# Operand sums, PSUM squares and weight portions in a kernel of attention and two feed-forward layers

## The chip, the cores and the metric

The kernel runs on one core of a Trainium2 chip. The metric is the device time of one execution in microseconds (us). TensorE (PE) multiplies matrices into eight PSUM banks, VectorE (DVE), ScalarE (ACT) and GpSimd (POOL) work element by element on SBUF and, the first two, on PSUM; SyncE (SP) issues DMAs.

## The reference

```python
def phi(x):                      # per batch and head, 128 random features
    proj = np.einsum('bhsd,md->bhsm', x, omega)
    h = proj - np.sum(x * x, axis=-1, keepdims=True) / 2.0
    h = h - np.max(h, axis=-1, keepdims=True)
    return np.exp(h) / np.sqrt(m)
kv = einsum(phi(k), v);  z = sum(phi(k))
attn = (phi(q) @ kv) / (phi(q) @ z + 1e-06)        # 4 x 8 heads, 576 x 64
x = attn as (2304, 512)
h = x @ moe_w_in;   r = maximum(h, 0); x = (r * r) @ moe_w_out      # 512 x 2048, 2048 x 512
h = x @ moe2_w_in;  g = where(h > 0, h, exp(minimum(h, 0)) - 1);  out = g @ moe2_w_out
```

All in float32.

## The kernel before

Each float32 operand is kept as two limbs of a shorter format, high and low, and each product is three matmuls (high x high, high x low, low x high). A low limb is made by VectorE as full minus high (`minus`, L76; names gl, wl, t1l and so on), the high one by a cast on ACT.

The 2304 tokens stand in five blocks: 0 to 3 of 512 columns and B = 4 of 256. The 2048 hidden columns of each layer stand in four groups of four (GF = 4). Group 0 of the first layer is computed plainly and partly beside the attention stages, in steps of one hidden part: blocks 0 to 2 in halves of 256 columns, then block 3, then block 4. Step s runs `gemm1` (12 matmuls into ph; ACT makes r = relu(ph), L516, and gh = r², L517; VectorE gf = r*r, L520, and gl = gf - gh) and then `gemm2` of step s - 2 (12 matmuls from gh and gl into py, L540). After the fourth part the sum py is copied to a page ya in SBUF by VectorE (L551, L557). Weight work is put between: `make(n, c)` carries weight part n through five phases: cm on ACT (L132), which reads a loaded page st; L139 and L140 on VectorE into cv; L149 on VectorE and, for pairs of parts, four sums cs and cd on GpSimd (L166 to L169); the cast wh on ACT (L195, L179); wl on VectorE.

All other groups are "tours" over one block each, with seven products in the manner of Strassen. A tour runs `product` (L662) into the PSUM pages pa, pw and pb; ACT copies pb, vs and us (L827, L828, L833) and VectorE adds c22 = pb + vs and c21 = pw + us (L839, L842); the squares follow (L676 to L678), then `chunk` (py, L721) and the sum into ya (L737). The products need sums of the input blocks: GpSimd joins the two limbs of x to xf (L620) and forms t1 to t4, and d for block B (L591 to L597); ACT and VectorE split each into limbs, SP stores these to DRAM (L571), and `load_x` brings them back. The tasks stand in a list `later`, of which `prepare(n)` takes n at fixed places of the program. The engines run their instructions in the program's order; the order is written out by hand.

Of the kernel before, what the change touches and what calls it, by code (L numbers as in the profile page):

```python
# [8 lines left out]
F32 = mybir.dt.float32  # L9
# [8 lines left out]
def linear_attention_two_ffn_kernel(  # L18
# [47 lines left out]
    def page(shape, name, dt=F32):  # L66
        return pages.tile([P] + list(shape), dt, tag="page", name=name)
# [4 lines left out]
    def flat(t):  # L72
        return t.rearrange("p a b -> p (a b)")
# [421 lines left out]
    def gemm1(o, j, ahead):  # L495
        i, n0, n1 = o
        n = n1 - n0
        nm = f"0_0_{i}_{n0}_{j}"
        ih, il = need((0, j, 0))
        lower()  # L500
        cast()
        ph = psum(f"ph{nm}")
        m = 0
        for c in range(KD):
            cs = slice(c * P, (c + 1) * P)
            for wt, xt in ((ih, xh), (ih, xl), (il, xh)):
                nc.tensor.matmul(ph[:, :n], wt[:, cs], x_part(xt, i, c)[:, n0:n1], start=(m == 0), stop=(m == 3 * KD - 1))  # L507
                m += 1
        if o == order(0, 0)[-1]:
            n_dead[0] += 1  # L510
        gf = page([n], f"gf{nm}")
        gh = page([n], f"gh{nm}", F32R)
        gl = page([n], f"gl{nm}", F32R)
        r = page([n], f"r{nm}")

        nc.scalar.activation(out=r, in_=ph[:, :n], func=AF.Relu)  # L516
        nc.scalar.activation(out=gh, in_=r, func=AF.Square)  # L517
        make(ahead, 1)
        make(ahead, 2)
        nc.vector.tensor_tensor(out=gf, in0=r, in1=r, op=ALU.mult)  # L520
        minus(nc.vector, gl, gf, gh)
        for c in (3, 0, 4):
            make(ahead, c)
        g_t[o, j] = gh, gl
        prepare(1)

    def gemm2(o, j):
        i, n0, n1 = o
        n = n1 - n0
        oh, ol = need((0, j, 1))  # L530
# [13 lines left out]
        if o == order(0, 0)[-1]:  # L544
            n_dead[0] += 1
        if j < GF - 1:
            return
        if per == 2:
            for t in range(KD // per):
                ya = ya_t[i, n0 // HN, t] = page([W], f"ya0_{i}_{n0}_{t}")  # L550
                nc.vector.tensor_copy(out=ya, in_=y_t[t])  # L551
            return
        for t in range(KD):
            for l in range(2):
                if t % 2 == 0:
# [46 lines left out]
    def operands1(i):  # L602
# [3 lines left out]
        made = [(name, b[l, k]) for name, l, k in PARTS[i == B]] + found  # L606
        later.extend(lambda name=name, t=t: split(1, i, name, t) for name, t in made)

    def operands0(i):

        def piece(d, l, k):
            return [x_part(d, i, 2 * k + e)[:, l * HN:(l + 1) * HN] for e in range(2)]

        def joined():
            b = {}
            for l in range(1 if i == B else 2):
                for k in range(2):
                    b[l, k] = page([W], f"xf{i}_{l}_{k}")
                    for e, (h, o) in enumerate(zip(piece(xh, l, k), piece(xl, l, k))):
                        nc.gpsimd.tensor_tensor(  # L620
                            out=b[l, k][:, e * HN:(e + 1) * HN], in0=h.bitcast(F32), in1=o.bitcast(F32), op=ALU.add
                        )
            found_t[i] = terms(0, i, b)

        for name, l, k in PARTS[i == B]:
            keep(0, i, name, (piece(xh, l, k), piece(xl, l, k)))
        joined()

    found_t = {}

    def operands0_limbs(i, n):
        name, t = found_t[i][n]
        split(0, i, name, t)

    def idle():
        pass

    def load_x(tour, name):
        moe, g, k, i = tour
# [110 lines left out]
        if moe == 0 and g == NG - 1 and l == (i < B):  # L750
            operands1(i)

    AHEAD = (0, 1, 3, 5, 8)

    def weights(tour):

        moe, g, k, i = tour
        prepare(2)
        lim = min(len(parts), 2 * NF * moe + 2 * GF * (g + 1) + AHEAD[k])
        due = n_made[2] - n_made[3]  # L760
        n_cast = len(casts)
        for _ in range(due):
            make(lim, 3)
        for _ in range(n_cast):
            cast()
        while n_made[1] < lim:
            make(lim, 0)
            make(lim, 0)
            make(lim, 1)
        for _ in range(due):  # L770
            make(lim, 4)
        for _ in range(n_cast):
            lower()
        while n_made[2] < lim:
            make(lim, 2)

    def toured(before):

# [5 lines left out]
        for n, tour in enumerate(tours):  # L784
# [6 lines left out]
            if i == B:  # L791
                bank_e, bank_o = psum(f"pe{nm}"), psum(f"po{nm}")
                times(tour, bank_e, "a", 0, "u", True, False, True)
                times(tour, bank_e, "a", 1, "v", False, True, False)
                run(carried)
                weights(tour)
                earlier(0)
                act_a(tour, "11", bank_e)
                times(tour, bank_o, "b", 0, "u", True, False, True)
                times(tour, bank_o, "b", 1, "d", False, True, False)  # L800
                earlier(1)
                act_a(tour, "21", bank_o)
# [4 lines left out]
                prepare(2)  # L807
# [22 lines left out]
            weights(tour)  # L830
# [5 lines left out]
            prepare(2)  # L836
# [8 lines left out]
            prepare(2)  # L845
# [120 lines left out]
```

## Time and profile before

| | |
|---|---|
| Median of three runs | 950.0 us (948.54 to 952.68) |
| Profiled execution | 950.98 us |
| Its span; granted clock of TensorE, mean | 949.1 us; 0.992 |
| PE busy | 917.3 us (97%) |
| DVE busy | 703.4 us (74%) |
| ACT busy | 528.9 us (56%) |
| POOL busy | 261.9 us (28%) |

Busy times are sums over a whole execution and hide in which stretch an engine is late; the waits and the stretches in the section of rows below do not. A matmul counts as busy until its modelled end, so that the number of matmuls in a stretch says more than its busy time. Durations are those of one profiled execution.

### The profile page before, as it was taken

The page shows a single profiled execution, that of the slowest core. Times are in us where ns is not written, and L with a number is a line of the kernel's source. Part 1 is how long each engine was busy: PE and PEld are TensorE (multiplying, and loading weights), DVE is VectorE, ACT ScalarE, POOL GpSimd, SP SyncE. Part 2 cuts the span into 40 slices and gives each one's busy share as a digit, 9 for nine tenths or more (in the row PEclk, how much of TensorE's full clock was granted, in tenths as well). Part 3 has the DMA queues.
Part 4 walks back from the last instruction along what each step waited for, and adds up shares of the span by engine and source line. Part 5 has one row for each costly group of instructions (what it writes and reads, how often), then busy time and mean ns, then how long its engine had stood idle before and what let it go on. Part 6 is the DMA issues. An engine that isn't in the chain of part 4 may idle for free.

```text
span 949.1 us, 20503 instructions
## 1 busy us (share of the span) xinstructions
PE 917.3 (97%) x7731; PEld 856.1 (90%) x7731; DVE 703.4 (74%) x1170; ACT 528.9 (56%) x1126; POOL 261.9 (28%) x370
## 2 busy tenths in 40 slices
PE   8998999969989999999999999999999999999997
PEld 7887889958889999999999998998899889989896
DVE  5889886899775775477549899897678767976553
ACT  5988966424343444254335565766476637665551
POOL 7666643589201100110025323220022002100000
PEclk9999999999999999999999999999999999999999
DMA  9464430345899685467439655376466746654632
GB/s 249 140 171 117 134 112 2 92 153 201 277 365 347 209 290 188 159 229 266 179 94 372 234 199 190 129 237 233 156 222 197 291 155 213 207 192 137 207 122 78
DMA packets 122882, 183.86 MB, mean 194 GB/s; under 512 B 33952, under 2 KB 53408, under 8 KB 122784
## 3 DMA queue, kind: packets, MB, share of 16 engines
q1 hardware_dynamic: 115024, 156.97, 48.7%
q0 software_dynamic: 6912, 25.17, 8.1%
q8 instruction: 61, 1.00, 0.4%
q10 hardware_dynamic: 848, 0.43, 0.2%
q14 instruction: 37, 0.30, 0.1%
HBM read 145.29 MB, written 37.22 MB: 192 GB/s over the span
## 4 chain that ended last, share of the span: by engine, by line
PE 67%; DMA 4%; DVE 3%; issue 1%; SPq 1%; POOL 1%; ACT 1%; DVEq 0%; POOLq 0%; ACTq 0%
PE py L713 21%; PE py L721 14%; PE pb L662 12%; PE pa L662 8%; PE pw L662 7%; PE po L662 2%; PE pe L662 2%; DMA st<-in_moe_w_out_dram 1%; PE ph L507 1%; DMA xd10q<-qh 1%; DMA xst4h<-xd00t 1%; SPq L571 1%; DMA xsdl<-xd04d 0%; DMA xst3h<-xd00t 0%; PE py L540 0%
## 5 line engine op out<-in xcount | busy, mean ns | idle before, releaser
L76 DVE TENSOR_TENSOR gl<-gf,gh 128x512 fp32r<-128x512 f32 (+1 forms) x158 | 112.7, 714 | 16.0 <-ACT gh L695 11.7
L721 PE MATMUL py<-gh,wl 128*128 128x256 f32 x432 | 121.3, 281 | 0.0
L721 PE MATMUL py<-gh,wh 128*128 128x256 f32 x432 | 121.3, 281 | 0.0
L721 PE MATMUL py<-gl,wh 128*128 128x256 f32 x432 | 121.2, 281 | 0.0
L713 PE MATMUL py<-wh,gh 128*128 128x512 f32 x288 | 113.6, 394 | 0.0
L713 PE MATMUL py<-wh,gl 128*128 128x512 f32 x288 | 113.4, 394 | 0.0
L713 PE MATMUL py<-wl,gh 128*128 128x512 f32 x288 | 113.3, 394 | 0.0
L685 DVE SCALAR_TENSOR_TENSOR r<-r,t 128x512 f32<-128x512 f32 x72 | 51.3, 713 | 63.3 <-ACT t L684 63.3
L737 DVE TENSOR_TENSOR ya<-py,ya 128x512 f32<-128x512 f32 x108 | 70.7, 684 | 23.1 <-PE py L721 12.8
L721 PEld LDWEIGHTS py<-gl,wh 128*128 128x128 f32 x432 | 81.4, 188 | 0.0
L721 PEld LDWEIGHTS py<-gh,wl 128*128 128x128 f32 x432 | 81.4, 188 | 0.0
L721 PEld LDWEIGHTS py<-gh,wh 128*128 128x128 f32 x432 | 81.3, 188 | 0.0
L116 POOL DMA_DIRECT2D st<-in_moe_w_in_dram x24 | 18.3, 766 | 204.2 <-DVE cv L140 164.2
L695 ACT CAST gh<-gf 128x512 fp32r<-128x512 f32 x72 | 44.4, 616 | 51.0 <-DVE gf L686 50.9
L678 DVE TENSOR_TENSOR gf<-r 128x512 f32<-128x512 f32 x54 | 37.9, 713 | 41.3 <-ACT r L676 40.9
L713 PEld LDWEIGHTS py<-wh,gl 128*128 128x128 f32 x288 | 54.1, 188 | 12.8
L713 PEld LDWEIGHTS py<-wl,gh 128*128 128x128 f32 x288 | 54.1, 188 | 10.0
L713 PEld LDWEIGHTS py<-wh,gh 128*128 128x128 f32 x288 | 54.1, 188 | 9.9
L827 ACT COPY pb<-pa 128x512 f32<-128x512 f32 x28 | 16.0, 571 | 68.4 <-PE pa L662 68.3
L121 POOL DMA_DIRECT2D st<-in_moe_w_out_dram x24 | 13.3, 554 | 145.9 <-ACT cm L132 86.4
L140 DVE SCALAR_TENSOR_TENSOR cv<-st,cv 128x512 uint32<-128x512 uint32 x64 | 48.4, 756 | 2.2
L540 PE MATMUL py<-gl,wh 128*128 128x256 f32 (+1 forms) x128 | 38.9, 304 | 9.3 <-DVE gl L76 9.2
(886 smaller groups left out, 3063.6 us busy)
## 6 DMA issues: line engine op xcount, KB each, us to landing
st<-in_moe_w_in_dram POOLq DMA_DIRECT2D x24, 512.0 KB, 6.9
st<-in_moe_w_out_dram POOLq DMA_DIRECT2D x24, 512.0 KB, 4.3
vk<-in_v_dram SPq DMA_DIRECT2D x32, 128.0 KB, 4.5
st<-in_moe_w_in_dram SPq DMA_DIRECT2D x8, 512.0 KB, 4.0
st<-in_moe_w_out_dram SPq DMA_DIRECT2D x8, 512.0 KB, 3.8
out_dram<-ya SPq DMA_DIRECT2D x16, 256.0 KB, 2.4
ld0k<-in_k_dram SPq DMA_DIRECT2D x4, 256.0 KB, 5.1
ld0q<-in_q_dram SPq DMA_DIRECT2D x4, 256.0 KB, 5.0
```

The lines of the kernel that those rows point to most:

```text
L76: eng.tensor_tensor(out=out, in0=whole, in1=hi.bitcast(F32), op=ALU.subtract)
L116: queue.dma_start(out=t.rearrange("p (c f) t -> p c (f t)", c=KD), in_=w[:, f * 2 * P:(f + 1) * 2 * P].rearrange("(c p) f -> p c f", p=P),)
L140: nc.vector.scalar_tensor_tensor(out=t, in0=lo, scalar=29, in1=t, op0=ALU.logical_shift_right, op1=ALU.bitwise_or)
L540: nc.tensor.matmul(y, w[:, ts], a, start=j == 0 and m == 0 and t % per == 0, stop=j == GF - 1 and m == 2, skip_group_check=per > 1,)
L662: nc.tensor.matmul(y[:, pr * HN:(pr + 1) * HN], wt[:, ws], xs[v][:, e * HN:(e + 1) * HN], start=fresh and first and pr == 0 and m == 0, st ...
L678: nc.vector.tensor_tensor(out=gf, in0=r, in1=r, op=ALU.mult)
L685: nc.vector.scalar_tensor_tensor(out=r, in0=r, scalar=1.0, in1=t, op0=ALU.add, op1=ALU.mult)
L695: nc.scalar.copy(out=gh, in_=gf)
L713: nc.tensor.matmul(y_t[l, u], a[:, s0], w, start=first and pr == 0 and m == 0, stop=last and pr == 1 and m == 2,)
L721: nc.tensor.matmul(y_t[l, u][:, e * HN:(e + 1) * HN], w[:, ts], a[:, pr * HN:(pr + 1) * HN], start=first and pr == 0 and m == 0 and e == 0 ...
L737: nc.vector.tensor_tensor(out=ya_t[key], in0=y_t[l, u], in1=ya_t[key], op=ALU.add)
L827: nc.scalar.copy(out=b, in_=a)
```

## The change

Four things differ; the order of TensorE's instructions is the same in both kernels.

1. In `gemm1`, gf is max(ph, 0)*r in one VectorE operation that reads ph in PSUM. Weight phases 1 and 2 stand before gf in even steps only, phases 3, 0 and 4 behind it in odd steps (and in every step of the last two blocks); weight parts are made up to 16 ahead of the dead ones, not 13. `prepare` takes 0, 1 or 4 tasks.
2. The 22 copies of py to ya in group 0 stand on ACT.
3. The joins and differences are single tasks, done in place in pages xr (four a block), each with its limbs six tasks later. Those of block 3 are read back from DRAM (xrh, xrl, one more stored part) and joined during group 1. All stores of group 0's parts are issued first on SP.
4. In a tour the weight work is cut into four portions (two for block B) with two tasks of `later` behind each, and runs one part further ahead.

```diff
         nc.scalar.activation(out=gh, in_=r, func=AF.Square)
-        make(ahead, 1)
-        make(ahead, 2)
-        nc.vector.tensor_tensor(out=gf, in0=r, in1=r, op=ALU.mult)
+        odd = i < B - 1 and j % 2
+        if not odd:
+            make(ahead, 1)
+            make(ahead, 2)
+        nc.vector.scalar_tensor_tensor(out=gf, in0=ph[:, :n], scalar=0.0, in1=r, op0=ALU.max, op1=ALU.mult)
         minus(nc.vector, gl, gf, gh)
-        for c in (3, 0, 4):
-            make(ahead, c)
+        if odd or i >= B - 1:
+            for c in (3, 0, 4):
+                make(ahead, c)
         g_t[o, j] = gh, gl
-        prepare(1)
+        prepare(4 if i >= B - 1 else 1 if odd else 0)
...
-                nc.vector.tensor_copy(out=ya, in_=y_t[t])
+                nc.scalar.copy(out=ya, in_=y_t[t])
...
+    def kept0(i):
+        for name, l, k in PARTS[i == B] + ((("r", 1, 0),) if i in LATE else ()):
+            keep(0, i, name, (piece0(xh, i, l, k), piece0(xl, i, l, k)))
...
+        return reads(b10, b00) + [join(*b10), join(*b00)] + reads(b11) + [
+            (diff(b00, b10, b00), limb("t1", *b00)), join(*b11),
+        ] + reads(b01) + [
+            (diff(b10, b11, b10), limb("t3", *b10)), (diff(b11, b11, b00), limb("t2", *b11)), join(*b01),
+            (diff(b01, b01, b11), limb("t4", *b01)),
+        ]
...
-    AHEAD = (0, 1, 3, 5, 8)
+    AHEAD = (1, 2, 4, 6, 8)
...
+        firsts = [f for _ in range(fresh) for f in (phase(0), phase(1))]
+        highs = [phase(3)] * due + [cast] * n_cast
+        lasts = [phase(4)] * due + [lower] * n_cast
+        return merged(firsts, highs) + merged(lasts, [phase(2)] * fresh)
+
+    def slot(chores, left):
+        run(kept)
+        run(chores, -(-len(chores) // left))
+        run(later, 2)
...
-            weights(tour)
+            chores = chores_of(tour)
+            slot(chores, 4)
             earlier(0)
...
-                later.extend([sums0[0], idle, idle, sums0[B], sums0[1]] + limbs0[0] + [sums0[2]] + limbs0[B] + limbs0[1])
-                later.extend([sums0[3]] + limbs0[2] + limbs0[3])
+                for i in range(NB):
+                    kept0(i)
+                in_turn(sum((operands0(i) for i in [0, B] + list(range(1, B))), []), 6)
...
-            gemm1(o, j, min(n_dead[0] + 13, 4 * GF) if alone[0] else 0)
+            gemm1(o, j, min(n_dead[0] + 16, 4 * GF) if alone[0] else 0)
```

GpSimd's order where the sums of block 0 begin, before:

```order
L620 TENSOR_TENSOR xf_0_0_3378<-xh_0_531,xl_0_532 128x256
L620 TENSOR_TENSOR xf_0_0_3378<-xh_1_700,xl_1_701 128x256
L620 TENSOR_TENSOR xf_0_1_3381<-xh_2_864,xl_2_865 128x256
L620 TENSOR_TENSOR xf_0_1_3381<-xh_3_1024,xl_3_1025 128x256
L620 TENSOR_TENSOR xf_1_0_3384<-xh_0_531,xl_0_532 128x256
L620 TENSOR_TENSOR xf_1_0_3384<-xh_1_700,xl_1_701 128x256
L620 TENSOR_TENSOR xf_1_1_3387<-xh_2_864,xl_2_865 128x256
L620 TENSOR_TENSOR xf_1_1_3387<-xh_3_1024,xl_3_1025 128x256
L594 TENSOR_TENSOR t_0_0_3390<-xf_1_0_3384,xf_0_0_3378 128x512
L595 TENSOR_TENSOR t_0_0_3391<-xf_1_1_3387,t_0_0_3390 128x512
L596 TENSOR_TENSOR t_0_0_3392<-xf_1_1_3387,xf_1_0_3384 128x512
L597 TENSOR_TENSOR t_0_0_3393<-xf_0_1_3381,t_0_0_3391 128x512
```

And the same place after the change:

```order
L633 TENSOR_TENSOR xr_1_0_3438<-xh_0_531,xl_0_532 128x256
L633 TENSOR_TENSOR xr_1_0_3438<-xh_1_700,xl_1_701 128x256
L633 TENSOR_TENSOR xr_0_0_3517<-xh_0_531,xl_0_532 128x256
L633 TENSOR_TENSOR xr_0_0_3517<-xh_1_700,xl_1_701 128x256
L166 TENSOR_TENSOR cs_5_3563<-cv_4_0_3472,cv_5_0_3557 128x256
L167 TENSOR_TENSOR cv_5_0_3557<-cv_5_0_3557 128x256
L168 TENSOR_TENSOR cs_5_3563<-cv_5_0_3557,cv_4_0_3472 128x256
L169 TENSOR_TENSOR cd_5_3564<-cv_4_0_3472,cs_5_3563 128x256
L651 TENSOR_TENSOR xr_0_0_3517<-xr_1_0_3438,xr_0_0_3517 128x512
L633 TENSOR_TENSOR xr_1_1_3693<-xh_2_864,xl_2_865 128x256
L633 TENSOR_TENSOR xr_1_1_3693<-xh_3_1024,xl_3_1025 128x256
```

The eight joins and four differences of block 0 stood in one row; now weight sums stand between them, and the differences overwrite the joined pages.

VectorE's order in group 0 before, from the second step of the second half of block 1 (the first index behind gf's layer and block is the first column, the next the step):

```order
L520 TENSOR_TENSOR gf_0_1_256_1_3466<-r_0_1_256_1_3469 128x256
L76 TENSOR_TENSOR gl_0_1_256_1_3468<-gf_0_1_256_1_3466,gh_0_1_256_1_3467 128x256
L551 COPY ya_1_0_0_3500<-py_0_1_0_0_3326 128x512
L551 COPY ya_1_0_1_3502<-py_0_1_0_1_3327 128x512
L76 TENSOR_TENSOR wl_4a<-cv_4_0_3429,wh_4a 128x512
L139 TENSOR_SCALAR cv_6_0_3527<-st_6_0_3432 128x512
L140 SCALAR_TENSOR_TENSOR cv_6_0_3527<-st_6_0_3432,cv_6_0_3527 128x512
L149 SCALAR_TENSOR_TENSOR cv_6_0_3527<-cm_6_0_3486,cv_6_0_3527 128x512
L520 TENSOR_TENSOR gf_0_1_256_2_3521<-r_0_1_256_2_3524 128x256
L76 TENSOR_TENSOR gl_0_1_256_2_3523<-gf_0_1_256_2_3521,gh_0_1_256_2_3522 128x256
L76 TENSOR_TENSOR wl_4b<-cv_5_0_3472,wh_4b 128x512
```

And after:

```order
L522 SCALAR_TENSOR_TENSOR gf_0_1_256_1_3507<-ph_0_1_256_1_3494,r_0_1_256_1_3510 128x256
L76 TENSOR_TENSOR gl_0_1_256_1_3509<-gf_0_1_256_1_3507,gh_0_1_256_1_3508 128x256
L76 TENSOR_TENSOR wl_4a<-cv_4_0_3472,wh_4a 128x512
L139 TENSOR_SCALAR cv_5_0_3557<-st_5_0_2269 128x512
L140 SCALAR_TENSOR_TENSOR cv_5_0_3557<-st_5_0_2269,cv_5_0_3557 128x512
L149 SCALAR_TENSOR_TENSOR cv_5_0_3557<-cm_5_0_3515,cv_5_0_3557 128x512
L522 SCALAR_TENSOR_TENSOR gf_0_1_256_2_3551<-ph_0_1_256_2_3538,r_0_1_256_2_3554 128x256
L76 TENSOR_TENSOR gl_0_1_256_2_3553<-gf_0_1_256_2_3551,gh_0_1_256_2_3552 128x256
L522 SCALAR_TENSOR_TENSOR gf_0_1_256_3_3600<-ph_0_1_256_3_3587,r_0_1_256_3_3603 128x256
L76 TENSOR_TENSOR gl_0_1_256_3_3602<-gf_0_1_256_3_3600,gh_0_1_256_3_3601 128x256
L76 TENSOR_TENSOR wl_4b<-cv_5_0_3557,wh_4b 128x512
```

The copies of ya are gone from the row, the weights stand between every second pair of gf and gl, and gf names ph.

ACT's order at the start of the first tour, before:

```order
L195 CAST wh_6_1_4438<-cv_6_1_4430 128x512
L132 ACTIVATE cm_7_1_4440<-st_7_1_4379 128x512
L576 CAST t3h_3_4447<-t_0_3_4176 128x512
L827 COPY pb_4466<-pa_1_0_4482 128x512
L828 COPY vs_1_0_4485<-pw_1_0_4483 128x512
```

And after:

```order
L517 ACTIVATE gh_0_4_0_3_4391<-r_0_4_0_3_4393 128x256
L579 CAST t1h_2_4398<-xr_0_0_4296 128x512
L579 CAST t3h_2_4407<-xr_1_0_4250 128x512
L878 COPY pb_4429<-pa_1_0_4445 128x512
L879 COPY vs_1_0_4448<-pw_1_0_4446 128x512
```

The cm that reads a loaded weight page is no longer ahead of pb; two limbs of block 2's differences are.

## Rows read from the trace of the kernel before

**Rows 1.** Waits of PE, whole span: engine, line, waited for: us, times, longest.

```profile
PE py L540 <- DVE gl L76: 9.2, 5, 3.2
PE pb L662 <- ACT pb L827: 3.1, 1, 3.1
PE pb L662 <- DVE c L839: 2.0, 3, 1.0
...
PE pb L662 <- ACT us L833: 1.7, 1, 1.7
```

**Rows 2.** Stretches: us, then PE, PEld, DVE, ACT, POOL busy (instructions), PEclk, DMA, GB/s.

```profile
175.00:185.00 10.00, 10.00 (x87) 10.00 (x86) 7.68 (x16) 4.61 (x10) 1.64 (x2) 1.00 0.34 88
185.00:195.00 10.00, 9.58 (x80) 9.17 (x78) 9.62 (x13) 5.08 (x11) 7.38 (x8) 1.00 0.87 292
195.00:205.00 10.00, 5.78 (x42) 5.57 (x43) 9.65 (x12) 2.87 (x6) 9.65 (x10) 0.94 0.37 121
205.00:215.00 10.00, 6.00 (x38) 5.50 (x38) 9.80 (x11) 3.48 (x8) 9.92 (x9) 0.84 0.28 105
215.00:225.00 10.00, 9.39 (x69) 9.18 (x69) 9.66 (x10) 3.87 (x10) 9.92 (x10) 0.88 0.57 198
...
265.00:275.00 10.00, 7.37 (x49) 7.37 (x50) 5.29 (x9) 5.53 (x10) 0.75 (x1) 0.83 0.96 337
400.00:450.00 50.00, 50.00 (x426) 50.00 (x425) 36.94 (x61) 24.88 (x42) 7.99 (x11) 1.00 0.71 246
500.00:550.00 50.00, 46.35 (x385) 45.52 (x384) 44.81 (x68) 28.09 (x51) 18.52 (x17) 1.00 0.81 296
```

**Rows 3.** Timeline of PE: start, us, operation, [idle before <- releaser].

```profile
267.63 0.39 PE L662 MATMUL pb<-xst2h,wh_4c 128*128 128x256 f32 x1 [3.13 <-ACT pb L827]
...
268.74 0.42 PE L662 MATMUL pb<-xst2h,wl_6c 128*128 128x256 f32 x1
...
271.95 0.33 PE L662 MATMUL pa<-xsph,wl_6a 128*128 128x256 f32 x1
```

**Rows 4.** Timeline of DVE in the stretch 193 to 211.

```profile
193.09 0.41 DVE L139 TENSOR_SCALAR cv<-st 128x512 uint32<-128x512 uint32 x1
...
194.95 0.42 DVE L520 TENSOR_TENSOR gf<-r 128x256 f32<-128x256 f32 x1
...
202.20 1.22 DVE L76 TENSOR_TENSOR wl<-cv,wh 128x512 fp32r<-128x512 f32 x1
...
210.28 0.68 DVE L76 TENSOR_TENSOR wl_6b<-cv,wh_6b 128x512 fp32r<-128x512 f32 x1
210.88 1.48 DVE L520 TENSOR_TENSOR gf<-r 128x256 f32<-128x256 f32 x1
```

**Rows 5.** Timeline of POOL beside it.

```profile
198.82 8.36 POOL L620 TENSOR_TENSOR xf<-xh,xl 128x256 f32<-128x256 f32 x8
207.14 1.48 POOL L594 TENSOR_TENSOR t<-xf,xf 128x512 f32<-128x512 f32 x1
```

**Rows 6.** One line's instructions: count, ns min/median/max, first and last start, forms.

```profile
L520 DVE TENSOR_TENSOR gf<-r x32: 407/426/1503, 124.5 to 262.7; 128x256 f32<-128x256 f32 x28, 128x512 f32<-128x512 f32 x4
...
L551 DVE COPY ya<-py x14: 672/676/685, 152.2 to 275.3; 128x512 f32<-128x512 f32 x14
...
L839 DVE TENSOR_TENSOR c<-pb,vs x28: 677/690/693, 275.9 to 913.5; 128x512 f32<-128x512 f32 x28
...
L620 POOL TENSOR_TENSOR xf<-xh,xl x36: 727/919/1193, 160.5 to 235.2; 128x256 f32<-128x256 f32 x36
```

**Rows 7.** Timeline of ACT in stages B and C.

```profile
265.93 0.66 ACT L132 ACTIVATE cm<-st 128x512 f32<-128x512 f32 x1 [2.51 <-DMA st<-in_moe_w_out_dram]
...
512.05 1.23 ACT L132 ACTIVATE cm<-st 128x512 f32<-128x512 f32 x2
513.19 0.57 ACT L833 COPY us<-pb 128x512 f32<-128x512 f32 x1
```

**Rows 8.** The page's DMA issues: count, KB each, median us to landing.

```profile
st<-in_moe_w_in_dram SPq DMA_DIRECT2D x8, 512.0 KB, 4.0
```

More of the change, by code (lines that the diff above doesn't have):

```diff
@@ L556, in gemm2 @@
                     ya_t[i, l, t // 2] = page([W], f"ya0_{i}_{l}_{t // 2}")
-                nc.vector.tensor_copy(
+                nc.scalar.copy(
                     out=ya_t[i, l, t // 2][:, t % 2 * HN:(t % 2 + 1) * HN], in_=y_t[t][:, l * HN:(l + 1) * HN]
@@ L607, in operands1 @@
         later.extend(lambda name=name, t=t: split(1, i, name, t) for name, t in made)
-    def operands0(i):
[L611 to L636, printed above, removed]
+    def piece0(d, i, l, k):
+        return [x_part(d, i, 2 * k + e)[:, l * HN:(l + 1) * HN] for e in range(2)]
+    xr, tt = {}, nc.gpsimd.tensor_tensor
+    def kept0(i):
+        for name, l, k in PARTS[i == B] + ((("r", 1, 0),) if i in LATE else ()):
+            keep(0, i, name, (piece0(xh, i, l, k), piece0(xl, i, l, k)))
+    def joined(i, l, k):
+        t = xr[i, l, k] = page([W], f"xr{i}_{l}_{k}")
+        if i == B:
+            tt(out=t, in0=flat(xh[B, k]).bitcast(F32), in1=flat(xl[B, k]).bitcast(F32), op=ALU.add)
+        elif i in LATE:
+            h, o = x_r.pop((i, l, k))
+            tt(out=t, in0=h.bitcast(F32), in1=o.bitcast(F32), op=ALU.add)
+        else:
+            for e, (h, o) in enumerate(zip(piece0(xh, i, l, k), piece0(xl, i, l, k))):
+                tt(out=t[:, e * HN:(e + 1) * HN], in0=h.bitcast(F32), in1=o.bitcast(F32), op=ALU.add)
@@ new lines, in linear_attention_two_ffn_kernel, with read, limbs, minus_of @@
+    LATE, x_r = (3,), {}
+    NAMES = {(0, 0): "b", (0, 1): "p", (1, 1): "q", (1, 0): "r"}
+    def read(i, l, k):
+        if i not in LATE:
+            return
+        x_r[i, l, k] = [page([W], f"xr{s}{i}_{l}_{k}", F32R) for s in "hl"]
+        for v, t in enumerate(x_r[i, l, k]):
+            nc.sync.dma_start(out=t.bitcast(F32), in_=xd[0, i, NAMES[l, k]][:, v, :])
+    def operands0(i):
+        def limbs(name, l, k):
+            split(0, i, name, xr.pop((i, l, k)))
+        def minus_of(o, a, b):
+            tt(out=xr[(i,) + o], in0=xr[(i,) + a], in1=xr[(i,) + b], op=ALU.subtract)
+        def reads(*ps):
+            return [lambda p=p: read(i, *p) for p in ps] if i in LATE else []
+        def join(*p):
+            return lambda: joined(i, *p)
+        def diff(*p):
+            return lambda: minus_of(*p)
+        def limb(name, *p):
+            return lambda: limbs(name, *p)
+        if i == B:
+            return [join(0, 0), join(0, 1), (diff((0, 1), (0, 1), (0, 0)), limb("d", 0, 1))]
+        b00, b01, b10, b11 = (0, 0), (0, 1), (1, 0), (1, 1)
+        return reads(b10, b00) + [join(*b10), join(*b00)] + reads(b11) + [
[4 more added lines that the diff above has]
+        ]
@@ L638, in load_x, with in_turn @@
+    def in_turn(tasks, lag):
+        due = []
+        for t in tasks + [None] * lag:
+            if isinstance(t, tuple):
+                due.append((len(later) + lag, t[1]))
+                t = t[0]
+            if t is not None:
+                later.append(t)
+            while due and (due[0][0] <= len(later) or t is None):
+                later.append(due.pop(0)[1])
     def load_x(tour, name):
@@ L751, in summed, with chores_of, phase, merged @@
             operands1(i)
-    AHEAD = (0, 1, 3, 5, 8)
-    def weights(tour):
+    AHEAD = (1, 2, 4, 6, 8)
+    def chores_of(tour):
         moe, g, k, i = tour
-        prepare(2)
         lim = min(len(parts), 2 * NF * moe + 2 * GF * (g + 1) + AHEAD[k])
[L760 to L775, printed above, removed]
+        due, n_cast, fresh = n_made[2] - n_made[3], len(casts), lim - n_made[2]
+        def phase(c):
+            return lambda: make(lim, c)
+        def merged(a, b):
+            return [f for m in range(max(len(a), len(b))) for f in a[m:m + 1] + b[m:m + 1]]
+        firsts = [f for _ in range(fresh) for f in (phase(0), phase(1))]
[6 more added lines that the diff above has]
+        run(later, 2)
     def toured(before):
@@ L795, in toured @@
                 run(carried)
-                weights(tour)
+                chores = chores_of(tour)
+                slot(chores, 2)
                 earlier(0)
@@ L806, in toured @@
                 act_b(tour, "21")
-                prepare(2)
+                slot(chores, 1)
                 earlier(3)
@@ L829, in toured @@
             run(carried)
-            weights(tour)
+            chores = chores_of(tour)
+            slot(chores, 4)
             earlier(0)
@@ L835, in toured @@
             act_a(tour, "11", a)
-            prepare(2)
+            slot(chores, 3)
             earlier(1)
@@ L844, in toured @@
             act_a(tour, "22", c22)
-            prepare(2)
+            slot(chores, 2)
             earlier(2)
@@ L851, in toured @@
             act_b(tour, "21")
-            prepare(2)
+            slot(chores, 1)
             earlier(3)
@@ L870, in moe_pieces @@
                 queued = True
-                sums0 = [lambda i=i: operands0(i) for i in range(NB)]
-                limbs0 = [[lambda i=i, n=n: operands0_limbs(i, n) for n in range(4 if i < B else 1)] for i in range(NB)]
-                later.extend([sums0[0], idle, idle, sums0[B], sums0[1]] + limbs0[0] + [sums0[2]] + limbs0[B] + limbs0[1])
-                later.extend([sums0[3]] + limbs0[2] + limbs0[3])
+                for i in range(NB):
+                    kept0(i)
+                in_turn(sum((operands0(i) for i in [0, B] + list(range(1, B))), []), 6)
             if o == order(0, 0)[-1] and j == 0:
```

## The prediction

> **What bounds the kernel now.** I read the list of waits of TensorE first, since the page gives it 97% of the span: any gain must come out of its idle time or its low clock. The reader is to see that five waits on gl make up 9.2 us, that one wait on the ACT copy pb has 3.1, and that products in the tours wait 2.0 on c and 1.7 on us [rows 1]; the rest of the list, some 10 us, lies in the attention stages, which the change leaves as they are. Then the busy time by stretch, to see what surrounds these waits [rows 2]. A stretch without waits issues 87 matmuls of 256 columns in 10 us (0.115 us each) or, in the tours, 426 in 50 us (0.117).
>
> Stage A is 185 to 225, the last of the halves in group 0. Its four windows hold 80 + 42 + 38 + 69 = 229 matmuls, which need 229 x 0.115 = 26.3 us; they take 40. So 13.7 us are lost: 9.2 in the five waits, the rest at a clock of 0.84 to 0.94 and in refilling. VectorE is busy 9.6 to 9.8 of each 10 us there, GpSimd 7.4 to 9.9. Stage B is the wait of 3.13 us on pb at 267.63, and behind it 16 matmuls spaced 0.214 instead of 0.117, from 268.74 to 271.95, while the granted clock is low: 16 x 0.097 = 1.5, so 4.6 us in all [rows 3]. Stage C is 500 to 550, with 385 matmuls where a full stretch has 426: 41 x 0.117 = 4.8 us. Together 23.1 us can be won, no more.
>
> **Why VectorE is late in A.** Its timeline shows the same operation at two lengths: wl 0.68 when GpSimd is between operations, 1.22 beside a burst of joins, gf 0.42 and 1.48 [rows 4]. GpSimd ran eight joins of 128x256 as one burst of 8.36 us there, and four differences behind it [rows 5]. By form, r*r in SBUF spreads from 407 to 1503 ns, but the ya copy from PSUM only from 672 to 685 and c = pb + vs, with one operand in PSUM, from 677 to 693 [rows 6]. So an operation with two operands in SBUF loses about 1.22 - 0.68 = 0.54 us for each GpSimd operation that it meets, and one that reads PSUM loses nothing. I take 0.52 us a GpSimd operation; the bounds are nothing and the length of a join itself, about 0.92 us at the median. The Trainium skill (page "SBUF — State Buffer", section "Who interferes with whom") says that a VectorE instruction with two SBUF inputs contends with a GpSimd instruction that reads SBUF, one with at most one SBUF input does not, and that the loser fully blocks. The first half is what the forms show; the second, the whole join as price, stands against my 0.52 and is the first rival's.
>
> **The change part by part.** (1) gf = max(ph,0)*r from PSUM: 32 of them, same count and shape. No row has max and product in one operation on a PSUM operand; the nearest, c = pb + vs of 512 columns, is 690 ns at the median and the plain copy from PSUM 676 [rows 6], so the second operand costs 14 ns at most, and I book a clean gf as before; bounds 0 and 0.2 us for the twelve in A. It can no longer be stretched: 12 in A by up to 0.53. Its PSUM page is held until VectorE has read it, not until ACT's relu has. That costs nothing while VectorE is less than a step late.
>
> (2) 22 ya copies go from VectorE to ACT. Fourteen of 676 ns, six of them in A (start to start 0.64): 3.8 us off VectorE there. On ACT each costs about 0.57, as the copy us does [rows 7]; ACT is busy 2.9 to 5.1 of 10 us in A, so they are hidden.
>
> (3) Operand sums. In the twelve steps from gf_0_1_256_0 to gf_0_2_256_3, TensorE needs 12 x 24 x 0.117 = 33.7 us. Before, VectorE had in these steps also seven limbs and six ya copies, of which none is left there by the order of after: it has 12 gf and 12 gl (24 x 0.45 = 10.8 with issue), six weight triples of 1.86 (193.09 to 194.95 in [rows 4]) = 11.2, and nine wl x 0.65 = 5.9, in all 27.9 us. GpSimd's operations in these steps fall from 37 in the four windows [rows 2] to about 18; the rest now lies in later steps and group 1. 18 x 0.52 = 9.4, so VectorE needs at most 37.3 us against 33.7. But the stretching also hits weight work, which is not urgent, and gl has room: four groups of 12 matmuls (5.6 us) lie between its ph and its use, its own chain of relu, gf and gl takes about 3 x 0.42 by a clean gf, so 4.3 us are free. 37.3 - 33.7 = 3.6 is inside that. I keep 1.5 us for steps where a triple and a diff meet, and book 12.2 of the 13.7; bounds 4 and 13.7.
>
> A step moved is its DMAs too: kept0 issues all stores of group 0 on SP at once, and the weight load st_6_0 now stands behind them. Such loads land after 4.0 us at the median [rows 8]; cm_6_0 on ACT and cv_6_0 on VectorE wait for it, and gf of the next step stands behind cv on VectorE. I book 0, bound 3 us.
>
> (4) Weights in four portions. In B, cm stood 2.51 us on a load right before pb [rows 7]; in after the two instructions before pb are t1h_2 and t3h_2, limbs that wait for GpSimd's differences of block 2. If GpSimd keeps up they are ready in time, so the wait goes and the next late thing is that difference. I book all 4.6; bounds 2 and 4.6. In C a row of casts and cm (512.05 the last) stood ahead of us at 513.19 [rows 7]; portions a quarter as long leave at most two or three ahead. I book 4.0 of the 4.8; bounds 1 and 4.8.
>
> (5) What it adds: in the first tours of group 1 GpSimd sums blocks 2 and 3, about 24 operations, where it had next to nothing (0.75 of 10 us at 265 [rows 2]). Times 0.52 that is up to 12 us of VectorE over four tours; c = pb + vs and the sums into ya read PSUM and are immune, squares and gl of the tours are not. VectorE is busy 37 of 50 us in a stretch of tours without waits, 400 to 450 [rows 2], so 13 are free. I book 2 us of new waits, each with a stretch of low clock behind; bounds 0 and 10.
>
> **Sum.** 950.98 (profiled; its span of 949.1 and 1.9 around it) - 12.2 - 4.6 - 4.0 + 2 = 932.2. The profiled execution is 1.0 above the median of the runs, so the median would be 931 by the same step; I say 932.
>
> **Rivals.** First, collisions at the full price: a join stops VectorE for its own length (the rule of that page, taken strictly). 18 x 0.92 = 16.6, VectorE 44.5 us against 33.7 + 4.3, so 6.5 us of waits stay in A with some 1.5 of slow clock, and 2 more in group 1 as its 24 operations lose 22 instead of 12: 942. For it speaks the gf of 1.48 (1.06 over), against it that most show 0.35 to 0.54.
>
> Second, the waits only move: A and B go, but in the four tours of group 1 with GpSimd's sums, limbs stand in front of pb and us on ACT, and one wait the size of B's (4.6 with its slow clock) arises in each: 4 x 4.6 = 18.4, so 932 - 2 + 18 = 948. It speaks for it that ACT is in order and that B itself was such a wait; against it, that each limb stands six tasks behind its difference.
>
> Third, slower: ACT behind GpSimd. The limbs of blocks 0 to 3 and B (17 casts) and three casts of weight sums stand in ACT's order in front of relu, gh and pb. If the differences come late by a mean of w, all 20 push TensorE's next operand by w. It decides from 23.1/20 = 1.2 us each; at 1.6, the length of one difference (1.48) just begun, 950.98 + 32 - 23.1 = 960. In A, ACT has 5 of 10 us free, which speaks against.
>
> That the change does not do what it says can be left out, since the orders of the engines show each part of it. A late st_6_0, by the 3 us of its bound, gives 935 and lies in the forecast's own range.
>
> **Chances.** Forecast 932, own range 927 to 938: 0.57. First rival 0.19 (938 to 945), second 0.13 (945 to 953), third 0.08; faster than every bound 0.03: the bounds end at 950.98 - 23.1 = 927.9, or 926.9 against the median. The range that leaves out 2 in 10 is 926 to 947. No change is within 0.5% (4.75 us, 945.2 to 954.7), about what a measurement here can tell: faster 0.79, same 0.13, slower 0.08.
>
> **What would show it.** In the waits of TensorE, py <- gl falls from 9.2 to under 2, pb <- pb is gone, c and us are under 1.5 together; 185 to 225 holds over 300 matmuls at clock 1.00; gf has a maximum near its minimum though GpSimd works beside it; POOL's busy time in 225 to 300 rises. It is wrong if py <- gl stays over 5 us (first rival), if a wait pb <- pb or pb <- us of over 3 us stands in a tour of group 1 (second), or if ACT's idle before t1h to t4h, released by GpSimd, precedes TensorE's waits (third).

## The result and the profile after

The changed kernel takes 934.09 us at the median of four runs (932.86 to 935.12), the kernel before 949.62 beside it; the ratio is 0.9831, 95% interval 0.9804 to 0.9857. The prediction was 932, its range 926 to 947. The profiled execution took 932.86 us. The page's head and the waits of TensorE after, in the columns of [rows 1]:

```profile
span 931.0 us, 20496 instructions
...
PE 911.8 (98%) x7731; PEld 852.2 (92%) x7731; DVE 690.1 (74%) x1148; ACT 539.2 (58%) x1148; POOL 253.7 (27%) x364
```

```profile
PE py L543 <- DVE gl L76: 2.5, 2, 2.0
...
PE pb L711 <- DVE c L891: 1.6, 2, 1.3
...
PE pb L711 <- ACT pb L878: 0.8, 1, 0.8
```

The 9.2 us on gl are 2.5, the 3.1 on pb 0.8, the 2.0 on c 1.6, and the 1.7 on us is gone. The stretches that answer to [rows 2], same columns:

```profile
185.00:195.00 10.00, 10.00 (x87) 10.00 (x86) 7.82 (x13) 5.14 (x12) 6.43 (x7) 1.00 0.51 181
195.00:205.00 10.00, 10.00 (x87) 10.00 (x87) 8.00 (x12) 6.05 (x14) 6.13 (x6) 1.00 0.17 57
205.00:215.00 10.00, 8.99 (x63) 8.06 (x61) 9.42 (x14) 5.56 (x12) 4.63 (x5) 1.00 0.22 64
215.00:225.00 10.00, 8.56 (x48) 7.45 (x49) 9.55 (x16) 4.09 (x8) 1.87 (x2) 1.00 0.48 162
...
500.00:550.00 50.00, 49.65 (x420) 49.44 (x419) 49.07 (x67) 28.10 (x51) 17.80 (x15) 1.00 0.72 250
```

From 205 on some of the matmuls counted are those of block 3, twice as wide, so their number alone says less there. GpSimd has 20 operations where it had 37. Its sums are later: in 225 to 300 it is busy 46.8 us instead of 20.7.

TensorE's order is the same in both kernels, so the start of the same matmul can be compared. The lead of the changed kernel, in us, at six matmuls (their starts from the two timelines):

| matmul | before | after | lead |
|---|---|---|---|
| py in group 0, ahead of stage A | 177.63 | 175.74 | 1.89 |
| ph of block 3, behind most of stage A | 227.45 | 212.66 | 14.79 |
| pw of the first tour | 261.51 | 249.37 | 12.14 |
| pe of the second tour | 278.64 | 263.81 | 14.83 |
| py, ahead of stage C | 491.25 | 476.75 | 14.50 |
| py, behind stage C | 555.10 | 536.56 | 18.54 |

So the stretch of stage A gives 12.9 us and loses 2.3 at one place, B gives 3.9 and loses 1.2 behind it, C gives 4.0. The first 1.9 are from the attention stages, which are the same in both kernels. In the profiles of the other kernels below, with the same attention stages, the lead at this matmul lies between -0.2 and 2.3, so it is chance.

The 2.3 lost at the end of A are one operation. VectorE's and GpSimd's timelines (start, us, operation):

```profile
212.66 0.42 DVE L522 SCALAR_TENSOR_TENSOR gf<-ph,r 128x256 f32<-128x256 f32 x1
213.18 3.21 DVE L76 TENSOR_TENSOR gl<-gf,gh 128x256 fp32r<-128x256 f32 x1
216.31 0.41 DVE L522 SCALAR_TENSOR_TENSOR gf<-ph,r 128x256 f32<-128x256 f32 x1
```

```profile
212.58 0.97 POOL L116 DMA_DIRECT2D st<-in_moe_w_in_dram  x1 [1.65 <-issue]
213.57 1.31 POOL L651 TENSOR_TENSOR xr<-xr,xr 128x512 f32<-128x512 f32 x1
214.81 1.28 POOL L627 TENSOR_TENSOR xr<-xh,xl 128x512 f32<-128x512 f32 x1
```

gl, 0.42 when clean, stands until a DMA issue and two sums of GpSimd are over. The gf on either side of it, which read PSUM, are clean (0.42 and 0.41). The wait that is left in front of pb is on ACT:

```profile
252.02 0.62 ACT L579 CAST t3h<-xr 128x512 fp32r<-128x512 f32 x1 [2.85 <-POOL xr L651]
252.54 0.58 ACT L878 COPY pb<-pa 128x512 f32<-128x512 f32 x1
```

### The profile page after: what moved, and what is told of

The parts are those of the page before. It is cut to its first block, busy times and chain, and to the rows that moved or that the text cites. A ratio compares the mean times of both kernels' runs of the same rounds, so it can differ in the third digit from the quotient of the medians.

```text
span 931.0 us, 20496 instructions
## 1 busy us (share of the span) xinstructions
PE 911.8 (98%) x7731; PEld 852.2 (92%) x7731; DVE 690.1 (74%) x1148; ACT 539.2 (58%) x1148; POOL 253.7 (27%) x364
## 4 chain that ended last, share of the span: by engine, by line
PE 77%; DVE 10%; ACT 6%; POOL 3%; DMA 2%; issue 2%; SPq 0%; DVEq 0%; POOLq 0%; ACTq 0%
PE py L762 21%; PE py L770 15%; PE pb L711 12%; PE pa L711 8%; PE pw L711 8%; PE ph L507 3%; PE py L543 2%; PE pe L711 2%; PE po L711 2%; POOL xr L633 1%; DVE cv L149 1%; POOL xr L651 1%; DVE cv L140 1%; DVE cv L139 1%; ACT ph0q L358 1%
## 5 line engine op out<-in xcount | busy, mean ns | idle before, releaser
L76 DVE TENSOR_TENSOR gl<-gf,gh 128x512 fp32r<-128x512 f32 (+1 forms) x158 | 110.1, 698 | 14.8 <-DMA xd02t<-t2h 5.2
L786 DVE TENSOR_TENSOR ya<-py,ya 128x512 f32<-128x512 f32 x108 | 69.9, 682 | 13.1 <-PE py L762 7.7
L166 POOL TENSOR_TENSOR cs<-cv,cv 128x256 f32<-128x256 f32 x14 | 14.5, 1038 | 211.5 <-DVE cv L149 131.7
L140 DVE SCALAR_TENSOR_TENSOR cv<-st,cv 128x512 uint32<-128x512 uint32 x64 | 53.7, 839 | 2.2
L885 ACT COPY us<-pb 128x512 f32<-128x512 f32 x28 | 16.4, 587 | 56.3 <-issue 30.2
```

The source lines that it names most:

```text
L76: eng.tensor_tensor(out=out, in0=whole, in1=hi.bitcast(F32), op=ALU.subtract)
L140: nc.vector.scalar_tensor_tensor(out=t, in0=lo, scalar=29, in1=t, op0=ALU.logical_shift_right, op1=ALU.bitwise_or)
L786: nc.vector.tensor_tensor(out=ya_t[key], in0=y_t[l, u], in1=ya_t[key], op=ALU.add)
```

## The experiments

Times are compared by ratio to the kernel before, run beside each on the same chip; 0.0010 of it is 0.95 us. My theory was that VectorE's operations with two operands in SBUF meet GpSimd's operations in stage A, and that fewer meet after the change. The rival was that VectorE merely had too many instructions there.

**Squares from SBUF again.**

```diff
-        nc.vector.scalar_tensor_tensor(out=gf, in0=ph[:, :n], scalar=0.0, in1=r, op0=ALU.max, op1=ALU.mult)
+        nc.vector.tensor_tensor(out=gf, in0=r, in1=r, op=ALU.mult)
```

> The changed kernel with gf = r*r read from SBUF again, all else as changed. Theory of collisions (VectorE operations with two SBUF inputs wait for GpSimd): the 128x256 gf spread again from 0.42 to 1 us and more, VectorE falls up to 0.5 us a step behind in 185 to 225, and the time is 935 to 939 us. Theory of amount (VectorE had only too many instructions in that stretch, GpSimd does not matter): no difference, 934 us, and gf stays near 0.42.

938.83 us, ratio 0.9892 (0.9873 to 0.9912): 5.8 us worse than the changed kernel's 0.9831. Single gf are stretched again, in the columns of [rows 6], first this run, then the changed kernel:

```profile
L522 DVE TENSOR_TENSOR gf<-r x32: 412/426/1772, 124.8 to 255.3; 128x256 f32<-128x256 f32 x28, 128x512 f32<-128x512 f32 x4
```

```profile
L522 DVE SCALAR_TENSOR_TENSOR gf<-ph,r x32: 408/424/685, 123.2 to 248.7; 128x256 f32<-128x256 f32 x28, 128x512 f32<-128x512 f32 x4
```

The maximum of 685 is that of the four with 512 columns; all with 256 columns stay at 0.42 or 0.43. Only part of the 5.8 is in gl's waits in group 0 (4.9 against 2.5); a further 2.3 is a wait on gl in a tour at 278, where VectorE had stood 7.8 us. In stage A itself only two gf are stretched, by 0.53 each, and the stretch takes 0.8 us longer than in the changed kernel (last table of this section). So this run shows that gf is free of GpSimd when it reads PSUM, but not that this is worth 5.8 us in stage A.

**Copies back on VectorE.** The two `nc.scalar.copy` of `gemm2` are `nc.vector.tensor_copy` again.

> The changed kernel with the 22 copies of ya back on VectorE. Six of them (3.8 us) stand in the stretch 185 to 225. Theory of collisions: VectorE's need there goes from some 37 to 41 us against 33.7 + 4.3 free, so 3 us of waits on gl come back: 936 to 940. Theory of amount: the copies were a sixth of the surplus of 13.7, and the time is 936 as well, but the gl waits would be as long without any stretched operation. If the copies' cost was hidden on either engine: 934.

937.65 us, 0.9879 (0.9863 to 0.9894): 4.6 us worse. The waits on gl in group 0 are 5.0, and the copies of block 3 now hold PSUM pages that TensorE needs (0.9 us in three small waits). Stage A takes 2.3 us longer. It fits both theories.

**Weight work of a tour in one piece.** `weights(tour)` and `prepare(2)` of the kernel before in place of the portions, and its AHEAD.

> The changed kernel with the weight work of a tour in one piece again, as before the change, and the old lead of one part less. By my step on the portions the waits at the end of group 1's last tours (before 500 to 550, 4.8 us) come back, and a wait on a load ahead of pb in the first tour (3 to 4.6 us): 939 to 943. Rival, that the operand sums and not the weight work had stood ahead of us, pb and c there: 934 to 936.

936.44 us, 0.9864 (0.9846 to 0.9883): 3.1 us worse by the point and less than expected, though the interval overlaps the changed kernel's. The trace settles the place:

```profile
PE py L543 <- DVE gl L76: 2.5, 2, 2.0
PE pb L711 <- ACT us L882: 2.0, 2, 1.8
PE pb L711 <- DVE c L888: 1.3, 2, 1.0
...
PE pb L711 <- ACT pb L876: 0.8, 1, 0.8
```

The waits of stage C are back; the long wait on pb of stage B is not. So the portions give C and not B. They also cost something: the changed kernel's wait of 1.3 us on c at 262 is missing here, with the same sums of GpSimd.

**Sums in one burst a block.** The first task of blocks 0, B, 1 and 2 makes all sums of its block, the others only the limbs.

```diff
-                in_turn(sum((operands0(i) for i in [0, B] + list(range(1, B))), []), 6)
+                in_turn(sum((burst(operands0(i), i) for i in [0, B] + list(range(1, B))), []), 6)
```

> The changed kernel with GpSimd's sums of blocks 0, B, 1 and 2 made in one burst a block, at the place of the block's first task; the limbs, the squares, the copies and the weight work stand where they are. The number of GpSimd operations in each block's stretch is the same. Theory of collisions by number of operations met: about the same, 934 to 936, since as many operations meet. Theory that the burst is what hurts (VectorE loses on every operation for 8 us and uses up the 4.3 us of room at once): 2 to 4 us for each of blocks 0 and 1, 938 to 943. Theory of amount: 934.

933.42 us, 0.9833 (0.9814 to 0.9852): the same as the changed kernel. The run does not do what it was meant to: block 0's burst now stands at 159 to 170 us, ahead of stage A, and block 1's behind 224, so stage A meets fewer operations than in the changed kernel, and whether a burst hurts by being one is not tested. In stage A there is no wait any more; instead a later one came, on a page that a store of limbs still holds, because the store stands behind 16 loads in SP's queue:

```profile
271.73 1.29 DVE L76 TENSOR_TENSOR gl<-gf,gh 128x512 fp32r<-128x512 f32 x2 [10.16 <-DMA xd02t<-t2h]
```

```profile
PE py L779 <- DVE gl L76: 3.2, 1, 3.2
```

**The old sums in the changed kernel.** The third item of the change is taken back as a whole: `operands0`, its stores and task list and one task a step are as before; all else as changed.

> The changed kernel with the operand sums of group 0 as before the change (whole blocks, B, 1 and 2 in the stretch 185 to 225, one task a step); squares from PSUM, copies on ACT, weight order and portions as changed. Theory of place (what helps is that the sums of blocks B, 1 and 2 no longer stand in that stretch, so fewer operations meet): 37 operations instead of 20 again, 5 to 8 us of gl waits come back: 937 to 941. Theory of amount (squares from PSUM and copies on ACT free VectorE enough): 932 to 934.

951.06 us, 1.0013 (1.0002 to 1.0024): the whole gain is gone, 17 us, three times what I expected. The waits on gl are 9.6 us and one on c 4.3. ACT shows a second way in which GpSimd's place matters: a cast of weights waits 7.35 us, because the weight sums stand in GpSimd's queue behind a block of joins. The relu behind that cast comes late by it, and TensorE waits 1.3 us on gh.

```profile
209.97 0.62 ACT L179 CAST wh_6b<-cv 128x512 fp32r<-128x512 f32 x1 [7.35 <-POOL cv L167]
```

**Two edits on the kernel before.** gf from PSUM and the copies on ACT, nothing else.

> The kernel before with two edits only: gf from PSUM and the copies of ya on ACT. The runs with each of these undone alone lost 6 and 5 us. Theory of amount: both give their 11 us, 938 to 939, with the wait on pb at 267 and the waits at 500 to 550 left as they were. Theory of place: the limbs and weights still meet 37 GpSimd operations, so half of the 13.7 stays: 942 to 945.

940.73 us, 0.9904 (0.9890 to 0.9919): 9.1 us better than before.

```profile
PE py L540 <- DVE gl L76: 5.2, 5, 2.1
PE pb L662 <- ACT us L833: 2.7, 1, 2.7
PE pb L662 <- DVE c L839: 1.4, 2, 1.0
```

The time lies between the two forecasts. More than half of stage A's waits on gl stay, and the stretch gains 4.1 us where the changed kernel gains 12.9, as the theory of place has it; stage C loses 1.6 more. But the wait on pb is gone, with no portion and no task moved. The load on which cm waited there is issued at 258.39 in the kernel before and at 250.08 here, 8.3 us earlier, while TensorE is only 5.0 ahead at the first pw (256.48 against 261.51). The load stands in SP's queue behind stores of low limbs that VectorE makes; the last of block 1, t4l, leaves at 240.37 before and at 231.96 here. So stage B looks like a late consequence of stage A; no run moves that load alone.

The same stretch of the program in each kernel, from the first to the second matmul of the table of leads; columns as in [rows 2], in the order before, two edits, old sums, changed, bursts:

```profile
177.63:227.45 49.82, 40.56 (x303) 38.98 (x301) 47.88 (x56) 20.59 (x45) 40.97 (x37) 0.93 0.52 173
```

```profile
176.69:222.45 45.76, 39.52 (x303) 37.81 (x301) 40.52 (x55) 23.50 (x51) 37.98 (x35) 0.96 0.56 186
```

```profile
175.91:225.97 50.06, 40.50 (x303) 39.34 (x301) 40.41 (x50) 23.33 (x51) 40.25 (x37) 0.93 0.59 187
```

```profile
175.74:212.66 36.92, 36.46 (x302) 36.00 (x301) 29.73 (x48) 20.20 (x45) 14.97 (x16) 1.00 0.41 137
```

```profile
176.03:212.22 36.19, 36.19 (x302) 35.91 (x301) 27.51 (x54) 21.52 (x47) 8.07 (x10) 1.00 0.48 155
```

TensorE's work is the same in all five. With 37, 35 and 37 operations of GpSimd beside it the stretch takes 49.8, 45.8 and 50.1 us; with 16 and 10 it takes 36.9 and 36.2. The pair of old sums and changed kernel decides against the theory of amount: VectorE has 50 and 48 instructions there, which by the shortest length of each form in their own traces would take 26.3 and 25.1 us, but it is busy 40.4 and 29.7. What grows is the length of the operations, not their number. In the run with old sums VectorE also stands idle for 10 of the 50 us, so the order of ACT behind GpSimd has a share in its loss.

**The lock measured by itself.** Stretches of twelve VectorE operations, alone and beside twelve of GpSimd.

> A kernel of its own that leaves the whole computation out and measures the disputed price: stretches of twelve VectorE operations of 128x512, alone, beside GpSimd adds of 128x256 and of 128x512, with one operand in PSUM beside such adds, with 256 columns, and beside GpSimd adds with a DMA issue before every two. By my price (about 0.5 us for each operation met, half of a join) the pairs of two engines take turns in part and 12 products of 0.68 beside 12 adds of 1.3 end within 16 us. By the full lock each waits for the other's whole operation: twelve products beside twelve adds of 128x512 take 12 x (0.6 + 1.3) = 23 us with a mean of about 1.8 each, and products of 256 columns wait as long. Both expect the form with an operand in PSUM at its clean length. A DMA issue in front is expected to let two GpSimd operations pass before VectorE's, up to 3 us for one operation, if it is what made the one gl of 3.21 us in the changed kernel.

By line and form: twelve's busy time, mean ns. L57 alone, L63 beside joins of 256 columns, L67 beside 512, L71 256 columns beside 512, L75 with an operand in PSUM beside 512.

```profile
L67 DVE TENSOR_TENSOR o<-a,b 128x512 f32<-128x512 f32 x12 | 18.0, 1568 | 2.5 <-ACT b L51 2.5
...
L71 DVE TENSOR_TENSOR o<-a,b 128x256 f32<-128x256 f32 x12 | 14.8, 1302 | 3.5 <-ACT b L51 3.5
L76 POOL TENSOR_TENSOR g<-a,c 128x512 f32<-128x512 f32 x12 | 14.7, 1272 | 1.8 <-ACT c L51 1.8
...
L63 DVE TENSOR_TENSOR o<-a,b 128x512 f32<-128x512 f32 x12 | 12.6, 1120 | 17.7 <-ACT b L51 17.7
...
L57 DVE TENSOR_TENSOR o<-a,b 128x512 f32<-128x512 f32 x12 | 7.3, 685 | 4.9 <-ACT b L51 4.9
L75 DVE SCALAR_TENSOR_TENSOR o<-z,b 128x512 f32<-128x512 f32 x12 | 7.3, 680 | 4.5 <-ACT z L51 4.5
```

The means hide that the first two products of a stretch ran before GpSimd began. By minimum, median and maximum, in the columns of [rows 6]:

```profile
L63 DVE TENSOR_TENSOR o<-a,b x12: 684/1205/1212, 29.9 to 41.3; 128x512 f32<-128x512 f32 x12
L64 POOL TENSOR_TENSOR g<-a,c x12: 717/1166/1238, 30.5 to 43.0; 128x256 f32<-128x256 f32 x12
L67 DVE TENSOR_TENSOR o<-a,b x12: 683/1744/1749, 44.9 to 61.1; 128x512 f32<-128x512 f32 x12
```

The two engines take turns. A product that meets an add of 256 columns, a join, loses 1205 - 684 = 521 ns, and one that meets an add of 512 columns 1744 - 683 = 1061. Alone these adds last 717 (the shortest of L64) and 1260 (the mean of twelve without VectorE), so the loss is the add's own length less 0.20 us in both cases. A form with an operand in PSUM loses nothing (680 beside 685), nor does it slow GpSimd (1272 beside 1260). The twelve products beside adds of 512 columns are busy for 18.0 us, between the 16 of my price and the 23 of the full lock. With a DMA issue of GpSimd ahead of every two sums, one product lasted 4.27 us, the length of two sums and most of two issues:

```profile
L79 DVE TENSOR_TENSOR o<-a,b x12: 678/1744/4271, 101.3 to 118.4; 128x512 f32<-128x512 f32 x12
```

**Weight phases in every step, lead of 13 parts.** The conditions on `odd` are dropped and 16 is 13 again.

> The changed kernel with the weight phases of group 0 in every step again and a lead of 13 parts, as before the change; squares from PSUM, copies on ACT, spread sums and portions as changed. If it is mattering that gf stands behind a triple of weights only in every second step: 2 to 4 us slower than the changed kernel, 936 to 938. If the room of 4.3 us covers either order: 933 to 934.

948.00 us, 0.9980 (0.9965 to 0.9994), 14 us worse: the expectation failed. Stage A has only 3.1 us of waits on gl, but with a low granted clock beside them (0.92 in 185 to 205) it takes 5.5 us longer than in the changed kernel. More is lost behind it: VectorE is busy only 10.1 of 20 us in 205 to 225 and gets the rest of the weights at 247 to 262, when GpSimd has sums again (11.3 of 17 us); pb waits 4.2 us, later gl and wl 4.3 together. Order and lead were undone at once, so the share of each is not known; the loss behind stage A speaks for the lead.

**Three versions on.** Block 0 alone in one burst (`if i: return tasks` in `burst`):

> The changed kernel with the sums of block 0 alone made in one burst, at the place of the block's first task (about 160 us, ahead of the late stretch); all others as changed. In the run with bursts in every block the waits on gl in 185 to 225 were gone and a later wait of 3.2 us on a gl page came in their place. Theory of place: the two gl waits (0.5 and 2.0) go and nothing is lost later, 930 to 931. Rival: the later wait comes with any earlier progress, since the DMA queues are full from 236 on, and the time stays 932 to 933.

929.13 us, 0.9778 (0.9762 to 0.9794): faster than the changed kernel, intervals apart, by 5.0 us. Stage A runs with no wait at all, pb does not wait either, and a gl page still waits 1.6. With lags of eight and seven tasks instead of six:

> As the kernel with the burst of block 0, and each pair of limbs eight tasks behind its difference, not six. In the changed kernel pb waits 0.8 us on ACT behind t3h of block 2, whose difference is late; with a lag of eight that limb stands behind pb. Expected 0.8 us under the kernel with lag six, 929 to 930. Rival: the limbs' stores leave later, their pages come free later, and a wait on a page takes as much: 931 to 934.

> The kernel with the burst of block 0 and a lag of seven tasks. With six a gl waited 1.6 us on a page, with eight c waited 2.0 us; between them one of the two remains: 929 to 931. If both go: 927.

930.74 us (0.9794, 0.9781 to 0.9808) and 930.55 (0.9800, 0.9781 to 0.9820): the gl page no longer waits, but c waits 2.0 and 2.3 us. Both intervals overlap that of the burst alone, so neither is shown to be slower or faster. With five tasks a step in the last two blocks:

> The kernel with the burst of block 0, and five tasks a step in the last two blocks of group 0, not four, so that the limbs of block 2 are made and stored ahead of the loads for the tour over block 4. The wait of 1.6 us on a gl page (held by a store of t2l that stands behind these loads) should go: 927 to 928. Rival: GpSimd is full from 225 to 256, so ACT waits for its differences that much earlier and pb or the copies of ya come late: 930 to 934.

932.78 us (0.9824, 0.9807 to 0.9842): its rival came true, pb waits 2.5 us on ACT. No one of the three beats the burst alone.

**Stretch by stretch.** TensorE's order is the same in all these kernels, so each can be cut at the same matmuls: those of the table of leads, and a py at 300.02 in the kernel before as the end of the second tour. Us gained on the kernel before in each stretch, from one profile each:

| kernel | stage A | rest of group 0 | first tour (B) | second tour | stage C |
|---|---|---|---|---|---|
| changed | 12.9 | -2.7 | 2.7 | 0.0 | 4.0 |
| squares from SBUF | 12.1 | -4.3 | 3.1 | -4.1 | 4.0 |
| copies on VectorE | 10.6 | -4.9 | 3.6 | -1.2 | 4.0 |
| weights in one piece | 12.9 | -2.6 | 4.3 | -0.1 | -0.7 |
| old sums | -0.2 | -3.5 | -0.7 | 0.0 | 4.0 |
| two edits alone | 4.1 | 0.0 | 5.4 | 0.1 | -1.6 |
| phases in every step | 7.4 | -0.1 | -1.4 | -7.1 | 4.1 |
| bursts | 13.6 | 0.0 | 2.7 | -5.0 | 4.1 |
| block 0 in a burst | 13.6 | -0.1 | 4.8 | -1.8 | 4.0 |

Once the sums are moved, squares from PSUM and copies on ACT are worth 0.8 and 2.3 us in stage A; the third item of the change, the sums, is worth 13.1 there, and order and lead of the weight phases 5.5. These do not add up: the 12.9 need several of them at once.

## Why the prediction was right, and where it was not

**Stage A** was booked at 12.2 of 13.7 us and gave 12.9 less 2.3, so 10.6. The step held in its mechanism: gf from PSUM was never stretched, the copies were hidden on ACT, and fewer operations met. The shares were not as told. Squares and copies taken back alone cost 0.8 and 2.3 us in stage A, and done alone they give 4.1 there; the place of the sums is worth nearly all, and without it nothing is left. My count of operations that meet was the right quantity. My price of 0.52 us was that of a join (0.52) and about half that of a sum of 512 columns (1.06). Over the stretch as a whole VectorE's operations in the changed kernel last 6.4 us more than the shortest of their forms, 0.4 for each of 16 operations of GpSimd, since not each is met. The 1.5 us kept for a triple and a difference that meet came as one wait of 2.0, behind a DMA issue that I had not priced. Four signs of the forecast were missed by little: gl waits 2.5 and not under 2, pb still waits 0.8, c waits 1.6 and not under 1.5, and 185 to 225 holds 285 matmuls and not over 300, as some of them are wide.

**The first rival** took the length of a join as the price. That was nearer than half of a join: a product that meets an add loses the add's own length less 0.20 us. But the 0.92 was the length of joins that were stretched themselves; alone a join lasts 0.72. The Trainium skill (page "SBUF — State Buffer", section "Who interferes with whom") says that a VectorE operation with two SBUF inputs contends with a GpSimd operation that reads SBUF, and that one with at most one SBUF input does not, outside what the page calls 2-port perf modes. The runs agree: 1205 and 1744 ns beside sums for two SBUF inputs, and 680 with one in PSUM, each against 685 for two SBUF inputs alone. My prediction left out the exception. `cv<-st` (L139) reads one SBUF page and is stretched all the same beside sums of GpSimd, to 0.96 us at 190.11 and 1.52 at 203.18, with 0.42 at the median:

```profile
L139 DVE TENSOR_SCALAR cv<-st x64: 410/422/1524, 24.8 to 810.1; 128x512 uint32<-128x512 uint32 x64
```

In which mode it runs, no trace here shows.

**Stage B** was booked whole at 4.6 and gave 3.9. The size was right by luck and the reason wrong: I gave it to the portions, but it goes with squares and copies alone, and stays gone without portions. The late thing that I named next, t3h behind GpSimd's difference, came, with 0.8 us.

**Stage C** was booked at 4.0 and gave 4.0, through the portions, as the run without them shows.

**The added work** was booked at 2 us over four tours. One wait of 1.3 us on c at 262 came in the first tour, with the granted clock at 1.00 and not low as I had booked; the later tours of group 1 lost nothing. What stood ahead of c is in VectorE's timeline:

```profile
257.00 2.48 DVE L727 TENSOR_TENSOR gf<-r 128x512 f32<-128x512 f32 x1 [1.27 <-ACT r L725]
259.40 0.41 DVE L139 TENSOR_SCALAR cv<-st 128x512 uint32<-128x512 uint32 x1
259.85 0.69 DVE L140 SCALAR_TENSOR_TENSOR cv<-st,cv 128x512 uint32<-128x512 uint32 x1
260.46 0.68 DVE L76 TENSOR_TENSOR t4l<-xr,t4h 128x512 fp32r<-128x512 f32 x1
261.06 0.68 DVE L891 TENSOR_TENSOR c<-pb,vs 128x512 f32<-128x512 f32 x1
```

gf, 0.68 when clean, is stretched beside a DMA issue and a sum of GpSimd, and behind it stand two operations of a weight portion. With the weights in one piece these two are not there, gf still lasts 1.84, and c does not wait. So the sums alone, which the booking named, did not make the wait; it came where they met the portions.

**The sum**: 950.98 - 10.6 - 3.9 - 4.0 + 1.2 - 1.9 (attention) = 931.8, measured 932.86, the difference being small losses between the places of the table and 0.5 behind them. The 1.9 are luck: the profiled executions differ by 18.1 us, the medians by 15.5, and by the medians the forecast was 2.1 us too low.

**The other rivals.** That the waits only move, to 948, is what the run with every-step weights did; the third rival's mechanism, ACT behind GpSimd, is real in the old sums' run, and its sign stands once in the changed kernel: ACT idle for 2.85 us before t3h, with 0.8 us of it passed on to TensorE. Neither decided in the changed kernel. What I had not seen is how far the edits depend on each other: the two edits alone give 9.1 us, everything but the new sums gives nothing (old sums: 1.0013), and everything but order and lead of the weight phases gives 1.9.

## What to carry to other kernels

Count, in the late stretch itself, the two-SBUF operations of VectorE and the operations of GpSimd beside them; move GpSimd's to where VectorE has room, before giving VectorE less work. An operand that is still in PSUM takes an operation out of this contest at no cost (424 ns beside 426 for gf, 680 beside 685). Undo edits one at a time before saying which gave what, and compare the starts of the same matmuls: here single undoings add up to far more than the gain, and much of what they cost lies in other stretches than the one that the edit was made for.

## What was not expected of the hardware

A DMA issue of GpSimd ahead of two of its sums let both pass a waiting VectorE operation: gl lasted 3.21 us instead of 0.42, at the same place in three other runs (3.20, 2.83, 3.20), and one product of 4.27 in the kernel that measures it alone, where the next issue of the same kind let one sum pass (2.23). Why the turn is lost there stays open. From 236 us on the DMA queues of the changed kernel are full (1.02 of their time in 235 to 245, at 374 GB/s), and a store of 256 KB behind loads holds its page so long that VectorE waited 10.2 us for it in the run with bursts.
